# One core, attention then a gated MLP: the first loads, the turning of P, and the sorting of the first batch's V are done another way

## The chip, the cores and the metric
The kernel runs on one core of one Trainium2 chip. A core has five engines that work at the same time, each through its own queue in the order in which its instructions were issued: TensorE (PE; its weight loads are shown apart as PEld), VectorE (DVE), ScalarE (ACT), GpSimd (POOL) and SyncE (SP, which here only issues DMAs). Transfers run on 16 DMA engines and are issued from SP's or POOL's queue. The metric is the time of one execution in microseconds; less is better. Three runs of the kernel before gave 181.19, 182.1 and 182.74 us.

## The reference
Two layers, one after the other. The inputs are q, k and v of shape (4, 8, 768, 64), that is 4 batches, 8 heads, 768 positions, head size 64, and `sort_net` of shape (4, 8, 8, 8): for each batch and head an 8x8 matrix over the 8 blocks of 96 positions.

```python
P = sort_net
for _ in range(5):
    P = P - np.max(P, axis=-1, keepdims=True)
    P = np.exp(P)
    P = P / (np.sum(P, axis=-1, keepdims=True) + 1e-09)
    P = P / (np.sum(P, axis=-2, keepdims=True) + 1e-09)
k_sorted = np.einsum('bhij,bhjcd->bhicd', P, k_b)      # blocks mixed by P
v_sorted = np.einsum('bhij,bhjcd->bhicd', P, v_b)
scores = scale * np.matmul(q_b, k_sb.transpose(0, 1, 2, 4, 3))   # inside each block
attn = softmax(scores)
x = matmul(attn, v_sb), heads side by side              # (4, 768, 512)

h = np.maximum(x @ w_in, 0.0)                           # 512 -> 1024
u, v = halves of h
v_n = (v - mean) / sqrt(var + 1e-06)
v_s = np.einsum('ts,bsd->btd', w_spatial, v_n) + b_spatial[None, :, None]
out = (u * v_s) @ w_out                                 # 512 -> 512
```

All inputs are fp32 and so is the output; the kernel multiplies in bf16.

## The kernel before
All work is cut into units, Python functions named `u_XX`, and one long string, `ORDER`, lists the units in the order in which they are issued. `SC:3:0:2:0`, say, calls `u_SC` with those arguments. Each engine takes its own instructions in that order, so `ORDER` is the schedule of all queues; engines wait for each other only through the data. Where a unit's first argument is a number, it is the PSUM buffer, one of four (`ps0` to `ps3`), that it uses; an `A`, `D` or `P` after it says whether ACT, DVE or POOL takes the result out of PSUM or does the elementwise work.

The head. `IN` issues the loads of `sort_net` (tile `p_all`, all 32 batches and heads on 32 partitions) and of the bias `b_spatial` (tile `b_bc`, on all partitions) from SP. `ID` makes the identity matrix on POOL and a small mask from it on DVE (`mask16`). `L:q`, `L:k`, `L:v` load one batch's q, k or v; these loads are issued by POOL, because they cast from fp32 to bf16 on the way. The first batch's q comes in two halves of 64 partitions. `L:wv`, `L:wu`, `L:ws`, `L:wo` load the weights in the same way. `SK` is one round of the normalisation of P: an `Exp` on ACT and six DVE operations (lines 191 to 207). In the last round P is written out expanded, 16 times along the free axis, into `p_x`, half by DVE and half by POOL. `PR` and `PS` turn P by eight matmuls of `p_x` with the identity (line 218) so that P stands with blocks on partitions. From this `P0` on DVE (line 227) makes `pd[0]`, and `PC` and `PD` (POOL, line 239) make `pd[1]` to `pd[3]`: for each head a 128x128 matrix that mixes blocks by P. `DM` are dummy matmuls on a tile of zeros; their results are not used.

Attention. Positions are laid out so that partition p of a tile holds the six positions 6p to 6p+5; a block of 96 positions is 16 partitions. Per batch and pair of heads (`hp`, 0 to 3), and for batch 0 per half of the blocks (`ih`, 0 or 1): `QT` transposes q by 12 matmuls with the identity (line 276); `KT` mixes and transposes k by 12 matmuls with `pd` (line 291); `VM` mixes v by two matmuls (line 313) into `vm`, which still has 16 partitions to a block. `VC` then copies `vm` into `vb`, where each block stands on partitions 0 to 95, by four DMAs on SP for each half (line 328); this is the only step by which V gets from one layout to the other. `SC` makes the scores of four blocks and two heads (eight matmuls, line 341) and ACT takes their `Exp` (line 349). `AT` multiplies by `vb` (eight matmuls, line 364), and DVE divides by the sum of each row (lines 371 and 372). `XT` transposes the result (line 386).

The MLP. `VP` and `UP` are the two halves of the first projection (lines 405 and 446), with relu on ACT or DVE; `LN` and `LA` normalise; `WS` transposes the spatial weights (line 255), six times 128 columns in all; `SP` multiplies by them (line 458), adds the bias on DVE (line 464) and gates with u on DVE or POOL (line 470); `OP` is the last projection (line 479), followed by the output's DMA on SP (line 487).

In `ORDER` the first `AT` of batch 0 stands soon after `VC:0:0` and `VC:0:1`, and the units of neighbouring batches are interleaved, so that attention of one batch runs among the MLP of the batch before.

Of the kernel before, what the change touches and what calls it, by code (L numbers as in the profile page):

```python
# [21 lines left out]
SC:2:0:3:0 QT:0:D:0:3:1 SC:3:0:1:0 AT:1:0:2:0 PD:1:0:4 QT:2:A:0:0:1 AT:0:0:0:0 SC:3:0:3:1 SC:1:0:1:1
AT:2:0:3:0 AT:0:0:1:0 SC:3:0:2:1 XT:1:D:0:0:1 L:wo SC:2:0:0:1 XT:3:D:0:0:0 AT:0:0:1:1 PD:1:4:8
AT:1:0:3:1 WS:2:A:1 L:v:2:0:128 VP:3:D:0:0:1 L:k:2:0:128 WS:0:A:3 VP:2:A:0:2 VM:1:A:1:2 VM:3:A:1:0
UP:0:A:0:0:0 VM:2:A:1:1 AT:1:0:2:1 UP:3:A:0:1:0 AT:0:0:0:1 KT:1:A:1:2:2 XT:2:D:0:1:1 VM:3:A:1:3
WS:0:D:2 KT:1:A:1:0:2 KT:2:D:1:1:2 KT:3:A:1:3:2 VC:1:0 PD:3:4:8 VC:1:1 WS:0:D:4 WS:1:D:0 QT:2:A:1:2:2
QT:3:D:1:3:2 QT:0:A:1:1:2 QT:1:D:1:0:2 SC:2:1:2:0 XT:3:D:0:1:0 SC:0:1:3:1 SC:1:1:2:1 AT:2:1:2:0
# [499 lines left out]
```

## Time and profile before
| | us |
|---|---|
| median of three runs | 182.1 (181.19 to 182.74) |
| the profiled execution's own time | 184.14 |
| its span, first to last instruction | 182.0 |
| PE busy | 154.3 |
| PEld busy | 95.9 |
| DVE busy | 117.2 |
| ACT busy | 90.7 |
| POOL busy | 35.2 |
| mean granted clock of TensorE, share of full speed | 0.937 |

The profile is that of one execution, in which the hardware wrote down each instruction's start and end. A line of it names an engine, the line of the kernel, the operation, the tile that is written and those that are read. An idle time is followed by what ended it (`<-`). A busy PE is not PE at its best: matmuls are pipelined, and the clock that TensorE is granted can be half of full speed. The share of DMA is a mean over 16 engines and may exceed one, since transfers overlap.

### The profile page before, as it was taken

The page shows a single profiled execution, that of the slowest core. Times are in us where ns is not written, and L with a number is a line of the kernel's source. Part 1 is how long each engine was busy: PE and PEld are TensorE (multiplying, and loading weights), DVE is VectorE, ACT ScalarE, POOL GpSimd, SP SyncE. Part 2 cuts the span into 40 slices and gives each one's busy share as a digit, 9 for nine tenths or more (in the row PEclk, how much of TensorE's full clock was granted, in tenths as well). Part 3 has the DMA queues.
Part 4 walks back from the last instruction along what each step waited for, and adds up shares of the span by engine and source line. Part 5 has one row for each costly group of instructions (what it writes and reads, how often), then busy time and mean ns, then how long its engine had stood idle before and what let it go on. Part 6 is the DMA issues. An engine that isn't in the chain of part 4 may idle for free.

```text
span 182.0 us, 4057 instructions
## 1 busy us (share of the span) xinstructions
PE 154.3 (85%) x1716; PEld 95.9 (53%) x1728; DVE 117.2 (64%) x244; ACT 90.7 (50%) x133; POOL 35.2 (19%) x41
## 2 busy tenths in 40 slices
PE   0097943999956999999999999999999999999670
PEld 0064732866843467667555666666556664556220
DVE  3356941758843399758887669996777846657600
ACT  3040750729973289782468673445582256720050
POOL 7606980400410000026300000300000330003000
PEclk9999985569997599999999999999999999999997
DMA  3999999999999970550903415400054000332054
GB/s 86 185 204 204 210 226 244 206 204 205 203 231 237 204 124 4 82 100 0 162 14 115 174 60 87 97 0 4 0 199 150 0 0 4 115 119 111 0 190 158
DMA packets 21921, 22.38 MB, mean 123 GB/s; under 512 B 1040, under 2 KB 18704, under 8 KB 21904
## 3 DMA queue, kind: packets, MB, share of 16 engines
q0 software_dynamic: 14864, 12.19, 42.7%
q1 hardware_dynamic: 7040, 9.94, 18.6%
q8 instruction: 13, 0.21, 0.4%
q14 instruction: 4, 0.03, 0.0%
HBM read 24.78 MB, written 6.29 MB: 171 GB/s over the span
## 4 chain that ended last, share of the span: by engine, by line
PE 68%; DMA 13%; DVE 6%; ACT 4%; SPq 4%; issue 2%; POOL 1%; ACTq 0%; DVEq 0%; POOLq 0%
PE ps L458 15%; PE ps L405 12%; PE ps L446 12%; PE ps L479 9%; DMA vb<-vm 8%; PE ps L364 5%; DMA q_in<-in_q_dram 4%; SPq L328 4%; PE ps L341 4%; PE ps L386 3%; PE ps L313 3%; PE ps L276 2%; PE ps L291 2%; DVE z L464 2%; DVE gt L470 2%
## 5 line engine op out<-in xcount | busy, mean ns | idle before, releaser
L458 PE MATMUL ps<-wspT,v_sb 128*128 128x384 bf16 x192 | 33.2, 326 | 0.0
L470 POOL TENSOR_TENSOR gt<-z,u_sb 128x768 bf16<-128x768 f32 x7 | 11.5, 1645 | 103.2 <-DVE z L464 78.2
L349 ACT ACTIVATE ex<-ps 96x768 bf16<-96x768 f32 x32 | 24.5, 804 | 11.4 <-PE ps L341 11.3
L405 PE MATMUL ps<-w_in_sb,xT 128*128 128x512 bf16 x88 | 25.0, 417 | 0.6 <-issue 0.2
L458 PEld LDWEIGHTS <-v_sb 128*128 128x128 bf16 x192 | 18.1, 98 | 11.5
L479 PE MATMUL ps<-w_out_sb,gt 128*128 128x512 bf16 x92 | 22.2, 380 | 1.8 <-DVE gt L470 1.7
L446 PE MATMUL ps<-xT,w_in_sb 128*128 128x384 bf16 x128 | 23.3, 326 | 0.0
L372 DVE TENSOR_TENSOR x_sb<-ps,rec 96x512 bf16<-96x512 f32 x32 | 22.0, 687 | 1.1
L364 PE MATMUL ps<-vb,ex 96*128 96x65 bf16 x256 | 14.9, 203 | 8.6 <-DMA vb<-vm 8.6
L419 DVE BATCH_NORM_STATS2 stats<-v_sb 128x6 f32<-128x512 bf16 x24 | 16.3, 678 | 5.7 <-ACT v_sb L110 5.4
L104 ACT COPY o_sb<-ps 128x1024 f32<-128x1024 f32 x11 | 11.1, 1012 | 17.3 <-PE ps L479 15.9
L464 DVE TENSOR_TENSOR z<-ps,b_bc 128x768 f32<-128x768 f32 x16 | 15.2, 952 | 6.6 <-PE ps L458 6.6
L364 PEld LDWEIGHTS <-ex 96*128 96x128 bf16 x256 | 12.4, 104 | 12.7 <-issue 6.4
L110 ACT ACTIVATE u_sb<-ps 128x768 bf16<-128x768 f32 x16 | 13.0, 811 | 12.3 <-PE ps L446 12.0
L371 DVE RECIPROCAL rec<-ps 96x8 f32<-96x8 f32 x32 | 6.3, 197 | 15.9 <-PE ps L364 15.6
L276 PE MATMUL ps<-ident,q_in 128*64 128x128 bf16 (+1 forms) x240 | 8.4, 221 | 9.0 <-DMA q_in<-in_q_dram 9.0
L446 PEld LDWEIGHTS <-w_in_sb 128*128 128x128 bf16 x128 | 11.9, 98 | 7.7
L479 PEld LDWEIGHTS <-gt 128*128 128x128 bf16 x96 | 8.8, 97 | 11.9 <-DVE gt L470 2.3
L405 PEld LDWEIGHTS <-xT 128*128 128x128 bf16 x96 | 9.4, 106 | 10.6 <-issue 2.9
L104 ACT CAST qT<-ps 128x768 bf16<-128x768 f32 (+1 forms) x13 | 8.4, 675 | 10.5 <-PE ps L276 10.4
L104 ACT CAST kT<-ps 128x768 bf16<-128x768 f32 (+1 forms) x13 | 9.4, 727 | 8.2 <-PE ps L291 8.2
L276 PEld LDWEIGHTS <-q_in 128*64 128x64 bf16 (+1 forms) x240 | 6.9, 120 | 9.5 <-DMA q_in<-in_q_dram 9.0
(63 smaller groups left out, 190.8 us busy)
## 6 DMA issues: line engine op xcount, KB each, us to landing
out_dram<-o_sb SPq DMA_DIRECT2D x12, 512.0 KB, 2.8
vb<-vm SPq DMA_DIRECT2D x32, 99.0 KB, 4.8
v_in<-in_v_dram POOLq DMA_DIRECT2D x4, 768.0 KB, 17.9
k_in<-in_k_dram POOLq DMA_DIRECT2D x4, 768.0 KB, 20.4
q_in<-in_q_dram POOLq DMA_DIRECT2D x3, 768.0 KB, 24.6
wsp_nat<-in_moe_w_spatial_dram POOLq DMA_DIRECT2D x1, 1152.0 KB, 23.6
w_in_sb<-in_moe_w_in_dram POOLq DMA_DIRECT2D x2, 512.0 KB, 16.6
q_in<-in_q_dram POOLq DMA_DIRECT2D x2, 384.0 KB, 10.7
```

What stands on the lines that cost most here:

```text
L104: nc.scalar.copy(out=out, in_=in_)
L276: nc.tensor.matmul(t[hh * 64:hh * 64 + 64, g * n:(g + 1) * n], lhsT=st["q", b][lo:lo + n, 2 * hp + hh, g * D:(g + 1) * D], rhs=ident[lo:lo ...
L349: nc.scalar.activation(out=e[:, 0:2 * NI * BLK].rearrange("p (h c) -> p h c", h=2), in_=t[0:BLK, :, 0:NI * BLK], func=AF.Exp, scale=scale,)
L364: nc.tensor.matmul(t[:, hh, ii * VW:ii * VW + D + 1], lhsT=e[:, c:c + 128], rhs=vb[b % 2][:, ih * NI + ii, 2 * hp + hh, 0:D + 1], start=Tr ...
L372: nc.vector.tensor_mul(out=x_sb[:, :, hp * 128:hp * 128 + 128].rearrange("p i (h d) -> p h i d", h=2), in0=tv[:, :, :, 0:D], in1=_raw_ap(r ...
L405: nc.tensor.matmul(t[:, x, :], lhsT=st["xT", b][:, kc, n * 128:(n + 1) * 128], rhs=w_in_sb[:, kc, DH:DFF], start=(kc == 0), stop=(kc == KC ...
L419: nc.vector.bn_stats(out=stats, in_=v_sb[:, x, :])
L446: nc.tensor.matmul(t[:, x, 0:HW], lhsT=w_in_sb[:, kc, mc * 128:(mc + 1) * 128], rhs=st["xT", b][:, kc, ih * HW:(ih + 1) * HW], start=(kc = ...
L458: nc.tensor.matmul(t[:, x, 0:HW], lhsT=st["v_sb", b, n][:, mc * 128:(mc + 1) * 128], rhs=wspT[:, n, x * HW:(x + 1) * HW], start=(n == 0), ...
L464: nc.vector.tensor_add(out=z.rearrange("p (x c) -> p x c", x=2), in0=t[:, :, 0:HW], in1=b_bc.rearrange("p (x c) -> p x c", x=2),)
L470: eng.tensor_mul(out=gt, in0=z, in1=st["u", b, mc // 2][:, mc % 2])
L479: nc.tensor.matmul(t[:, x, :], lhsT=st["gt", b, mc][:, c * 128:(c + 1) * 128], rhs=w_out_sb[:, mc, :], start=(mc == 0), stop=(mc == FC - 1),)
```

## The change
Five things change, and `ORDER` is written anew from end to end.

- The first 64 partitions of batch 0's q are loaded by SP as fp32 into a new tile, `q_raw`, and cast on chip by the new unit `CQ`, a pair of heads at a time: three pairs on POOL, one on ACT. The second half of q is loaded as before.
- The first loads that POOL issues are K and V of batch 0. The bias `b_bc` is no longer loaded in `IN` but by a unit of its own, `BB`, which stands among batch 1's attention.
- The last round of `SK` writes P once, as bf16, and DVE turns it in two blocks of 32x32 (`p_t`). `PR` then expands it by eight matmuls with a constant tile of selections, `sel`, which `SX` makes on POOL from the identity. `p_x`, the expansion by DVE and POOL, and `PS` are gone. The mask is made by a unit of its own, `MK`.
- For batch 0 alone, `VM` and `VC` are replaced by `VT` and `VX`. `VT` mixes and transposes V as `KT` does K (12 matmuls, and a copy of 128x384); `VX` transposes it back block by block (four transposes on TensorE and a copy of 96x512), which writes `vb` directly. Batches 1 to 3 keep `VM` and `VC`.
- There are 10 dummy matmuls instead of 20.

```diff
     def u_IN():
         nc.sync.dma_start(out=p_all, in_=sort_net.rearrange("b h i j -> (b h) i j"))
-        nc.sync.dma_start(
-            out=b_bc, in_=_raw_ap(moe_b_spatial, 0, [[0, 128], [1, S]]))
+        nc.sync.dma_start(out=q_raw, in_=_raw_ap(q, 0, [[G * D, 64], [S * D, H], [1, G * D]]))
...
+    def u_BB():
+        nc.sync.dma_start(out=b_bc, in_=_raw_ap(moe_b_spatial, 0, [[0, 128], [1, S]]))
+
+    def u_SX():
+        nc.gpsimd.tensor_copy(
+            out=sel.rearrange("p i (j t) -> p i j t", t=TB),
+            in_=_raw_ap(ident, 0, [[ident.ap[0][0], BH], [NB, NI], [1, NB], [0, TB]]),
+        )
...
+    def u_CQ(eng, hp):
...
+        o, i = st["q", 0][0:64, 2 * hp:2 * hp + 2], q_raw[:, 2 * hp:2 * hp + 2]
+        if eng == "A":
+            nc.scalar.copy(out=o, in_=i)
+        else:
+            nc.gpsimd.tensor_copy(out=o, in_=i)
...
+        nc.vector.tensor_mul(
+            out=p_bf if int(last) else p_all, in0=p_all,
+            in1=_raw_ap(colsum, 0, [colsum.ap[0], [0, NB], colsum.ap[1]]),
+        )
         if int(last):
-            for ih, eng in enumerate((nc.vector, nc.gpsimd)):
-                eng.tensor_mul(
-                    out=p_x[ih],
...
+            nc.vector.transpose(
+                out=p_t.rearrange("p x y -> p (x y)"), in_=p_bf.rearrange("p i j -> p (i j)"))
 
     def u_PR(ps):
         st["pr"] = ps_tile(ps)[:, :, 0:NI * BH].rearrange("p x (i y) -> p x i y", i=NI)
...
+        for ih in range(2):
+            for ii in range(NI):
+                nc.tensor.matmul(
+                    st["pr"][:, ih, ii, :], lhsT=sel[:, ii, :], rhs=p_t[:, ih, :], start=True, stop=True)
...
+    def u_VT(ps, eng, hp, ih):
+        hp, ih = int(hp), int(ih)
+        t = ps_tile(ps).rearrange("p x c -> p (x c)")
+        mix_T(t, st["v", 0], 0, hp, ih * 64, 64)
+        st["vT", hp, ih] = att.tile([128, HW], BF16, name="vT", tag="vT", bufs=3)
+        copy(
+            eng,
+            st["vT", hp, ih].rearrange("p (x g) -> p x g", g=G),
+            t[:, 0:HW].rearrange("p (g x) -> p x g", g=G),
+        )
+
+    def u_VX(ps, eng, hp, ih):
+        hp, ih = int(hp), int(ih)
+        t = ps_tile(ps, BF16)
+        for ii in range(NI):
+            nc.tensor.transpose(
+                t[0:BLK, 0, ii * 128:(ii + 1) * 128], st["vT", hp, ih][:, ii * BLK:(ii + 1) * BLK], ident)
+        copy(
+            eng,
+            vb[0][:, ih * NI:(ih + 1) * NI, 2 * hp:2 * hp + 2, 0:D],
+            t[0:BLK, 0, 0:NI * 128].rearrange("p (i h d) -> p i h d", i=NI, h=2),
+        )
```

The beginning of `ORDER` after the change, up to the last unit of batch 1's `VC` and the first `AT` that reads it, so that the units between them can be counted:

```
IN ID L:k:0:0:128 MK L:v:0:0:128 SX SK:0 L:wv SK:0 CQ:P:2 CQ:A:3 SK:0 QT:0:A:0:3:0 SK:0 QT:1:A:0:2:0
DM:2:5:384 CQ:P:1 CQ:P:0 SK:1 L:q:0:64:128 IV:1 QT:3:A:0:0:0 QT:0:D:0:1:0 DM:1:5:384 PR:2 IV:0 PC:A
P0:0:4:8 P0:0:0:4 KT:3:A:0:3:0 KT:1:A:0:0:0 P0:1:4:8 L:wu PD:2:0:4 VT:0:A:1:0 P0:1:0:4 KT:2:D:0:2:0
PD:3:0:4 KT:3:A:0:0:1 KT:1:D:0:3:1 VT:0:D:2:0 SC:2:0:0:0 VT:3:D:0:0 PD:3:4:8 L:ws KT:1:D:0:1:0
SC:0:0:3:0 VX:2:D:1:0 L:v:1:0:128 L:k:1:0:128 VX:3:D:0:0 SC:1:0:2:0 KT:0:D:0:2:1 KT:2:A:0:1:1
QT:3:D:0:2:1 QT:1:A:0:1:1 QT:0:D:0:3:1 VT:2:A:3:1 SC:3:0:1:0 VX:1:D:2:0 AT:0:0:0:0 PD:1:0:4
VT:2:A:3:0 QT:1:A:0:0:1 VT:3:D:0:1 L:q:1:0:128 SC:2:0:1:1 VX:0:D:3:0 L:wo AT:1:0:2:0 VX:3:A:0:1
VX:0:A:3:1 AT:2:0:3:0 VT:3:A:1:1 VT:1:A:2:1 L:v:2:0:128 AT:0:0:1:0 SC:3:0:2:1 XT:2:D:0:0:1 SC:1:0:3:1
XT:0:D:0:0:0 L:k:2:0:128 VX:3:A:1:1 PD:1:4:8 WS:2:D:1 SC:1:0:0:1 WS:0:D:3 VX:3:A:2:1 L:q:2:0:128
WS:2:D:0 AT:1:0:1:1 WS:0:A:5 AT:3:0:0:1 VP:2:D:0:0:1 VM:1:A:1:2 VM:0:A:1:1 UP:3:A:0:0:0 VM:2:D:1:0
VM:1:A:1:3 VP:0:A:0:2 KT:3:A:1:2:2 KT:1:A:1:0:2 AT:2:0:3:1 UP:0:A:0:1:0 AT:3:0:2:1 KT:1:A:1:3:2
VC:1:1 XT:2:D:0:1:0 KT:0:A:1:1:2 QT:3:D:1:0:2 QT:1:A:1:3:2 QT:2:D:1:2:2 VC:1:0 QT:0:A:1:1:2 WS:3:D:2
SC:1:1:3:1 XT:2:D:0:1:1 SC:0:1:2:1 SC:3:1:1:0 AT:1:1:3:1 VP:2:A:0:5 SC:0:1:3:0 AT:1:1:2:1
```

More of the change, by code (lines that the diff above doesn't have):

```diff
@@ L22 @@
[L22 to L27, printed above, removed]
@@ L142, in alloc, with load @@
         st[x, b] = ld.tile([128, H, G * D], BF16, name=f"{x}_in", tag=x)
-    def load(x, b, lo, hi, first):
+    def load(x, b, lo, hi):
         src = {"q": q, "k": k, "v": v}[x]
-        if first:
+        if (x, b) not in st:
             alloc(b, x)
@@ L154, in u_L @@
         if what in ("q", "k", "v"):
-            load(what, int(a[0]), int(a[1]), int(a[2]), int(a[1]) == 0)
+            load(what, *(int(x) for x in a))
         elif what == "wv":
```

81 lines of the change are left out of this document (33 added, 48 removed).

## The prediction
> **What bounds the kernel now.** I read the page first, for the span and the row of the clock that was granted to TensorE in 40 slices, then the waits (us in total, times, longest) and the chain in order of time (start, length).
>
> ```profile
> span 182.0 us, 4057 instructions
> ...
> PEclk9999985569997599999999999999999999999997
> ```
>
> ```profile
> PE ps L364 <- DMA vb<-vm: 8.6, 9, 1.6
> ```
>
> ```profile
> 1.25 7.74 DMA q_in<-in_q_dram
> ...
> 22.88 7.66 DMA vb<-vm
> ...
> 52.88 6.04 DMA vb<-vm
> ```
>
> The execution took 184.14 us: this span and 2.14 us around it. TensorE waits for data three times: for the first half of q until 8.99, and twice for `vb`, the sorted V that DMAs copy from `vm`. After both waits for `vb` the clock row falls to 5. A table by stages prices that (columns: stretch and its length, busy time of PE, PEld, DVE, ACT and POOL with counts, granted clock, DMA share, GB/s):
>
> ```profile
> 17.86:24.95 7.09, 6.43 (x172) 5.11 (x172) 6.42 (x13) 4.87 (x8) 6.60 (x8) 1.00 1.20 210
> 24.95:30.60 5.65, 0.69 (x4) 0.36 (x5) 0.25 (x1) 0.88 (x2) 1.92 (x2) 0.58 1.17 242
> 30.60:37.50 6.90, 6.90 (x110) 6.14 (x110) 5.07 (x12) 3.60 (x5) 2.04 (x2) 0.50 1.30 213
> 37.50:39.70 2.20, 1.98 (x9) 0.92 (x8) 1.03 (x3) 0.80 (x1) 0.00 (x0) 0.53 1.32 208
> 39.70:52.00 12.30, 12.18 (x205) 9.00 (x205) 10.29 (x19) 10.27 (x15) 2.92 (x3) 1.00 1.30 205
> 52.00:56.70 4.70, 1.55 (x18) 0.92 (x19) 0.68 (x3) 1.46 (x2) 0.00 (x0) 0.99 1.24 244
> 56.70:63.20 6.50, 5.96 (x32) 2.62 (x30) 2.62 (x6) 2.55 (x5) 0.00 (x0) 0.50 1.30 215
> 63.20:161.00 97.80, 97.12 (x1031) 59.41 (x1040) 74.57 (x143) 59.21 (x84) 10.75 (x7) 1.00 0.31 72
> ```
>
> From 63.2 to 161 PE is busy 97.12 of 97.80: there it is the bound, and only work taken from PE would help. Before 63.2 it loses 4.96 us idle in the second row, 3.15 in the sixth, and runs at half clock for some 15 us. What half clock costs is seen in one group of score matmuls (line 341) and in the V projection (line 405), each slow and fast:
>
> ```profile
> 50.59 0.38 PE L341 MATMUL ps<-qT,kT 64*96 64x96 bf16 x8
> ...
> 57.44 0.56 PE L341 MATMUL ps<-qT,kT 64*96 64x96 bf16 x8
> ...
> 59.83 3.62 PE L405 MATMUL ps<-w_in_sb,xT 128*128 128x512 bf16 x8
> ...
> 75.15 1.89 PE L405 MATMUL ps<-w_in_sb,xT 128*128 128x512 bf16 x7
> ```
>
> 0.38 to 0.56 is a factor 1.5; 0.27 to 0.45 a matmul is 1.7. Of a busy microsecond at half clock 0.33 to 0.41 comes back.
>
> **Part 1, the head: -1.7 us.** Everything waits for the first `KT` matmul, at 17.86 now. Its chain is the five rounds of `SK`, then P into `pd`.
>
> ```profile
> 1.20 0.41 SPq L169 DMA_DIRECT2D b_bc<-in_moe_b_spatial_dram  x1
> ...
> 5.06 0.26 ACT L191 ACTIVATE p_all<-p_all 32x64 f32<-32x64 f32 x1 [2.46 <-DVE p_all L205]
> ...
> 9.61 0.48 ACT L104 CAST qT<-ps 128x384 bf16<-128x384 f32 x1 [4.29 <-PE ps L276]
> 9.98 0.25 ACT L191 ACTIVATE p_all<-p_all 32x64 f32<-32x64 f32 x1
> ...
> 10.46 5.96 PE L248 MATMUL ps<-warm 128*128 128x384 bf16 x20
> ...
> 11.74 0.26 ACT L191 ACTIVATE p_all<-p_all 32x64 f32<-32x64 f32 x1 [0.41 <-DVE p_all L205]
> ...
> 17.86 0.38 PE L291 MATMUL ps<-pd,k_in 128*64 128x64 bf16 x12 [0.94 <-DVE pd L227]
> ```
>
> ```profile
> b_bc<-in_moe_b_spatial_dram SPq DMA_DIRECT2D x1, 384.0 KB, 5.1
> ```
>
> ```profile
> L470 POOL TENSOR_TENSOR gt<-z,u_sb 128x768 bf16<-128x768 f32 x7 | 11.5, 1645 | 103.2 <-DVE z L464 78.2 <-DVE rec L371 25.0
> ```
>
> A round takes 11.74 - 9.98 = 1.76. The third `Exp` stands on ACT behind a copy that waits for q, so it starts at 9.98 instead of about 6.8. After the change the same place holds `CQ:A:3`, which waits for `q_raw`: the chain still hangs on q. `q_raw` is 768 KB from SyncE; `b_bc`, half of that, from the same queue at the same moment took 5.1 from its issue at about 1.2. So it lands between 6.3 (no dependence on size) and 11.4 (twice 5.1); I take 9.0, near the middle. Then the cast on ACT (0.8, as ACT's copies of that length), three rounds to 15.1, the DVE turn (a 32x64 operation, about 0.25), four `PR` matmuls and a `P0`: first `KT` at 16.2. The other way in is POOL: three `CQ:P` of 768 elements, between ACT's 0.8 and the 1.645 of POOL's two-input product, after `q_raw`. PE's queue holds two `QT` that need them, five dummy matmuls (0.3 each, from the 20 in 5.96) and then `PR`. At 1.645 POOL is done at 13.9 and `PR` starts at about 16.1, `KT` at 17.0; at 1.1, which I take as a middle, it is hidden behind the rounds. Bounds for the first `KT`: 13.5 to 18.6, a gain of 4.4 to a loss of 0.7.
>
> [...]
>
> Queued behind `CQ` on POOL are q's second half, `wu`, then three `PD`, and only then `ws` and batch 1's loads; K and V ahead of it go earlier than now. `SX` delays only `wv`. `b_bc` moves behind batch 1's `VC` on SP, long before `SP` wants it: nothing.
>
> **Part 2, batch 0 until its first V projection: -1.6 us.** Now that stretch runs from 17.86 to 37.5, 19.6 us. The change takes out eight DMAs on SP and four `VM`, and puts in eight `VT` and eight `VX`. On PE that is eight groups of 12 small matmuls and eight of four transposes, 128 in all, about 4.0 us by the first stage row (172 in 6.43, of which the eight long ones of `VM` took some 1.3), less those 1.3: +2.7. All PE units of the new stretch come to some 13.5 at full clock, so PE no longer sets its length. DVE and ACT do:
>
> ```profile
> L349 ACT ACTIVATE ex<-ps 96x768 bf16<-96x768 f32 x32 | 24.5, 804 | 11.4 <-PE ps L341 11.3
> ...
> L372 DVE TENSOR_TENSOR x_sb<-ps,rec 96x512 bf16<-96x512 f32 x32 | 22.0, 687 | 1.1
> ...
> L106 DVE COPY xT<-ps 128x768 bf16<-128x768 bf16 x12 | 6.6, 553 | 2.4 <-PE ps L386 2.3
> L371 DVE RECIPROCAL rec<-ps 96x8 f32<-96x8 f32 x32 | 6.3, 197 | 15.9 <-PE ps L364 15.6
> ...
> L106 DVE CAST kT<-ps 128x384 bf16<-128x384 f32 x5 | 2.6, 553 | 0.5 <-PE ps L291 0.5
> ...
> L104 ACT CAST kT<-ps 128x384 bf16<-128x384 f32 x3 | 1.4, 480 | 4.5 <-PE ps L291 4.5
> ```
>
> In the new order DVE has, up to `VP:2:D:0:0:1`: nine 384-element copies (`KT`, `QT`, `VT`) of 0.553, four `VX` at two thirds of the `xT` copy, 0.4 (an estimate), five 768-element `XT` and `WS` copies of 0.553, six `AT` of 0.197 + 0.687, and three `P0` of about 0.42: 5.0 + 1.6 + 2.8 + 5.3 + 1.25 = 15.9. ACT has eight `Exp` of 0.804, eleven copies of 0.48, four `VX` of about 0.6, a `WS` of 0.8 and `PC` of 0.4: 15.3. In the first stage row, with nothing to wait for, DVE was busy 6.42 of 7.09, 91%; 15.9 at that share is 17.5, and with ACT nearly as full I take 18.0. Bounds: PE alone at 13.5 (a gain of 6.1), and 20.5 (a loss of 0.9) if the two engines wait on each other in turn. The 8.6 us of waiting for `vb` thus goes, but mostly into DVE and ACT; that is why the step is worth so little here.
>
> **Part 3, from there to 63.2: -8.5 us.** Here the waits of batch 1 stand.
>
> ```profile
> 46.99 0.80 ACT L104 CAST vm<-ps 128x768 bf16<-128x768 f32 x1
> ...
> 47.86 5.63 SPq L328 DMA_DIRECT2D vb<-vm  x8
> ...
> 55.95 0.31 PE L364 MATMUL ps<-vb,ex 96*128 96x65 bf16 x5 [0.52 <-DMA vb<-vm]
> ...
> 58.97 0.43 PE L364 MATMUL ps<-vb,ex 96*128 96x65 bf16 x5 [0.50 <-DMA vb<-vm]
> ```
>
> Batch 1's copies start when the last `VM` is evicted (47.79); the first half is all there 8.2 us later and the second 11.2. PE ran out of other work at 52, some 4 us after. In the new order, after the last `VM` (`VM:1:A:1:3`), PE still has a single `VP`, four `KT`, two `AT`, a `UP`, two `XT`, four `QT`, a `WS` and three `SC` before the first `AT` of batch 1: an estimated 7.6 us of PE work (1.3 the `UP`, 0.9 the `VP`, 0.3 to 0.4 each of the small groups), and 8.6 of ACT's (ten operations of 0.8 and a shorter one). So it arrives at 8 to 9, when the first half is there, and the second half is wanted 5 us later, at 13 against 11.2. Both waits go, and what followed them: idle 0.22 + 0.12 + 3.15 + 0.54 = 4.0, and half clock 0.41 x (1.98 + 5.96) = 3.2. Three `WS` groups (six matmuls each) have moved into Part 2, 1.3 on PE. Sum 8.5. DVE at 10.29 of 12.30 in the fifth row leaves room. Bounds: 2 (waits remain) to 9.5.
>
> **Part 4, loads and the rest: +1.3.** DMA is saturated until past 63 (share 1.2 to 1.3 in the stage rows).
>
> ```profile
> 31.78 0.94 POOL L148 DMA_DIRECT2D q_in<-in_q_dram  x1 [4.91 <-PE ps L276]
> ...
> 71.33 0.53 PE L276 MATMUL ps<-ident,q_in 128*64 128x128 bf16 x12
> ```
>
> ```profile
> q_in<-in_q_dram POOLq DMA_DIRECT2D x1, 768.0 KB, 28.3
> ```
>
> Batch 2's q now lands at 60.1 and is wanted at 71.33, 11 us of slack, which the gain eats. But batch 0's eight copies, 0.8 MB, are gone from that traffic, some 3 us at 205 GB/s and more, while q's first half as fp32 takes the place of `b_bc`; so it lands at about 57 and is wanted at about 58: +0.5, from 0 to +4. The rest holds the same PE work to 0.4 us. At the end the last gate now writes `gt` 0, which the first `OP` reads first, where now two matmuls of 0.22 go ahead of it: +0.4.
>
> **Sum.** -1.7 - 1.6 - 8.5 + 1.3 = -10.5: 173.6 against this execution's 184.14. That one lies 2.04 above the median of 182.1. The stretches at half clock, which the change removes, are the likeliest part to differ between executions, so the new kernel should stand nearer its own sum: 173.0.
>
> **Rivals.** (a) Batch 1 still waits for `vb`, because DVE or loads push `VM` late or because the copies land later: 6 us of Part 3 come back less a little, 178.5. For: the copies go out one by one, and end 11 us after the last `VM` now. Against: 8 us of cover where there were 4. Chance 0.12.
>
> (b) In Part 2 PE is busy only 13.5 of 18 us, in short pieces. The row 24.95:30.60 shows that the clock falls within such a stretch of little work. If it falls once late in Part 2, and takes the 9 us to come back that it took before (30.6 to 39.7), most of that lies in Part 3, where PE is close to the bound: 9 x 0.41 less a little, 176.5. Chance 0.10. [...] Against: 6.43 of 7.09 kept it at 1.00 in the first row.
>
> (c) The slower side: the clock falls early in Part 2 and, with gaps everywhere, doesn't return until the first units of batch 2 are through. Then Part 2 takes 13.5 x 1.5 = 20.3 instead of 18.0, Part 3, with 15.5 of PE work in 17.2, takes 15.5 x 1.7 = 26.4, and some 7 us of PE work behind it lose 4: +15.5, 188.5. It is slower than before from about 29 us of PE work at half clock on. Against: the fifth row shows 12 us at full clock right after a fall. Chance 0.05.
>
> (d) `q_raw` is starved behind K, V and `wv`, 2.1 MB at the 205 GB/s of the stage rows, and lands at about 17 instead of 9: +8, 181.0. Against: `b_bc` wasn't starved. Chance 0.04.
>
> (e) DVE and ACT overlap so well that PE sets Part 2: 13.5 + 0.5, 4.0 less: 169.0. Chance 0.07.
>
> **Numbers.** My forecast, 173.0, has 0.62; its own bounds are 169 to 177. The range 168 to 179 takes in (a), (b) and (e). About 1% is what a measurement tells from no change, 180.3 to 183.9. Faster: 0.62 + 0.12 + 0.10 + 0.07 = 0.91; same: (d), 0.04; slower: (c), 0.05.
>
> **What would show it.** Part 1: the first `KT` matmul near 16, `q_raw` landing near 9, `PR` released by DVE. Part 2: the first `VP` some 18 us after the first `KT`, DVE about 90% busy in between, no wait for `vb`, clock 1.00. Part 3: no wait over 1 us for `vb` in batch 1. Part 4: no wait for q or K of batch 2 over 1 us. I am wrong if the clock row shows 5 anywhere after the head, if `vb` stays among the longest waits of PE, or if the first `KT` comes after 18.6.

## The result and the profile after
The changed kernel takes 174.96 us, the median of four runs (173.83 to 175.95); the kernel before, run beside it, 182.42. The ratio is 0.960, with a 95% interval of 0.951 to 0.969. The forecast was 173.0, with a range of 168 to 179. Executions of one kernel differ by 1 to 3% here, and a trace is that of one of them; where a traced execution lies off its median, its own time is given. The traced one of the changed kernel took 175.73 (before: 184.14), with a span of 173.7 (182.0).

The page of the kernel after, its span and the row of the granted clock:

```profile
span 173.7 us, 4271 instructions
...
PEclk9999975569999999999999999999999999999996
```

The clock row still falls to 5 after the head, in one stretch instead of two, and this stretch stands where no wait for `vb` is. The head, in the timeline (start, length):

```profile
7.84 0.83 ACT L203 CAST q_in<-q_raw 64x768 bf16<-64x768 f32 x1 [3.48 <-DMA q_raw<-in_q_dram]
...
7.87 2.36 POOL L205 CAST q_in<-q_raw 64x768 bf16<-64x768 f32 x3 [3.20 <-DMA q_raw<-in_q_dram]
...
15.43 0.71 PE L303 MATMUL ps<-pd,k_in 128*64 128x64 bf16 x24 [0.92 <-DVE pd L239]
```

The first `KT` starts at 15.43 (17.86 before). The stages behind it, each row a stretch with its length, busy time of PE, PEld, DVE, ACT and POOL (with counts of instructions), granted clock, DMA share and GB/s:

```profile
15.43:20.11 4.68, 4.53 (x157) 3.94 (x157) 4.05 (x11) 3.66 (x7) 4.68 (x6) 1.00 1.27 206
20.11:21.81 1.70, 0.00 (x1) 0.00 (x1) 0.52 (x1) 0.43 (x1) 1.70 (x2) 1.00 1.24 207
21.81:26.64 4.83, 4.83 (x128) 4.23 (x128) 3.04 (x7) 3.85 (x7) 1.72 (x3) 0.75 1.16 212
26.64:27.73 1.09, 0.00 (x1) 0.00 (x0) 0.18 (x1) 0.05 (x1) 0.00 (x0) 0.50 1.23 199
27.73:37.87 10.14, 10.14 (x140) 9.28 (x139) 6.14 (x13) 5.70 (x10) 4.85 (x5) 0.50 1.31 204
37.87:54.79 16.92, 16.16 (x233) 10.48 (x233) 13.10 (x26) 13.30 (x20) 1.81 (x2) 1.00 1.26 228
54.79:157.00 102.21, 101.78 (x1066) 62.60 (x1074) 78.77 (x151) 59.64 (x84) 9.07 (x6) 1.00 0.40 91
```

Rows two and four are new: PE does nothing, and DVE and ACT do little (0.52 and 0.43 of 1.70 us, 0.18 and 0.05 of 1.09). The chain of waits names no releaser for them; "issue" is time in which the engine waited for nothing that the profile shows:

```profile
1.19 6.63 DMA q_raw<-in_q_dram
...
20.11 1.70 issue
...
26.64 1.09 issue
...
45.68 5.57 DMA vb<-vm
```

What was left of the waits for `vb`, 0.6 us, stands at the end of the row of its group:

```profile
L399 PE MATMUL ps<-vb,ex 96*128 96x65 bf16 x256 | 13.8, 201 | 1.7 <-issue 1.1 <-DMA vb<-vm 0.6
```

Part by part, in us of the two traces. Part 3 ends at the two groups of score matmuls that follow `VP:3:D:0:3:4` in both orders; they start at 63.38 before and at 54.79 after. (The prediction cut at 37.5 and 63.2, and so had 19.6 and 25.7 for Parts 2 and 3 before.)

| | before | predicted | after |
|---|---|---|---|
| Part 1, to the first `KT` | 17.9 | 16.2 | 15.4 |
| Part 2, to the first `VP` | 19.8 | 18.0 | 22.4 |
| Part 3, to these score matmuls | 25.8 | 17.2 | 16.9 |
| Part 4, to the end of the span | 118.6 | 119.9 | 118.9 |

Part 3 came as predicted; Part 2 became 2.7 us longer where 1.6 less was predicted. That is 4.4 more than the forecast and 1.9 beyond its outer bound of 20.5. The question is what stands in Part 2.

### The profile page after: what moved, and what is told of

It is laid out like the page before. It is cut to its first block, busy times and chain, and to the rows that moved or that the text cites. A ratio compares the mean times of both kernels' runs of the same rounds, so it can differ in the third digit from the quotient of the medians.

```text
span 173.7 us, 4271 instructions
## 1 busy us (share of the span) xinstructions
PE 151.8 (87%) x1827; PEld 97.8 (56%) x1838; DVE 120.1 (69%) x252; ACT 93.5 (54%) x140; POOL 34.1 (20%) x42
## 4 chain that ended last, share of the span: by engine, by line
PE 74%; DMA 9%; DVE 9%; issue 3%; ACT 2%; SPq 1%; ACTq 0%; DVEq 0%
PE ps L493 17%; PE ps L440 11%; PE ps L481 11%; PE ps L514 10%; PE ps L399 5%; PE ps L376 5%; DMA q_raw<-in_q_dram 4%; PE ps L303 3%; PE ps L421 3%; DMA vb<-vm 3%; PE ps L288 2%; PE ps L336 2%; PE ps L267 2%; DMA out_dram<-o_sb 2%; PE ps L348 1%
## 5 line engine op out<-in xcount | busy, mean ns | idle before, releaser
L384 ACT ACTIVATE ex<-ps 96x768 bf16<-96x768 f32 x32 | 24.7, 803 | 17.9 <-PE ps L376 17.5
L505 POOL TENSOR_TENSOR gt<-z,u_sb 128x768 bf16<-128x768 f32 x6 | 9.8, 1638 | 100.4 <-DVE z L499 76.6
L514 PE MATMUL ps<-w_out_sb,gt 128*128 128x512 bf16 x92 | 21.7, 379 | 2.3 <-DVE gt L505 2.1
L440 PE MATMUL ps<-w_in_sb,xT 128*128 128x512 bf16 x89 | 22.2, 379 | 0.4
L106 ACT COPY o_sb<-ps 128x1024 f32<-128x1024 f32 x10 | 10.1, 1013 | 18.4 <-PE ps L514 14.3
L112 ACT ACTIVATE u_sb<-ps 128x768 bf16<-128x768 f32 x15 | 12.1, 809 | 7.8 <-PE ps L481 7.4
L481 PEld LDWEIGHTS <-w_in_sb 128*128 128x128 bf16 x128 | 11.8, 98 | 7.6
L399 PE MATMUL ps<-vb,ex 96*128 96x65 bf16 x256 | 13.8, 201 | 1.7 <-issue 1.1
L440 PEld LDWEIGHTS <-xT 128*128 128x128 bf16 x96 | 8.7, 97 | 9.2
L376 PEld LDWEIGHTS <-kT 64*96 64x96 bf16 x256 | 8.2, 128 | 4.9 <-issue 3.7
L376 PE MATMUL ps<-qT,kT 64*96 64x96 bf16 x256 | 10.8, 219 | 0.1
L112 ACT ACTIVATE v_sb<-ps 128x1024 bf16<-128x1024 f32 (+1 forms) x9 | 8.4, 928 | 4.6 <-PE ps L440 4.6
```

The source lines that it names most:

```text
L112: nc.scalar.activation(out=out, in_=in_, func=AF.Relu)
L376: nc.tensor.matmul(t[0:BLK, hh, ii * BLK:(ii + 1) * BLK], lhsT=kT[rows, i * BLK:(i + 1) * BLK], rhs=qT[rows, i * BLK:(i + 1) * BLK], start ...
L384: nc.scalar.activation(out=e[:, 0:2 * NI * BLK].rearrange("p (h c) -> p h c", h=2), in_=t[0:BLK, :, 0:NI * BLK], func=AF.Exp, scale=scale,)
L399: nc.tensor.matmul(t[:, hh, ii * VW:ii * VW + D + 1], lhsT=e[:, c:c + 128], rhs=vb[b % 2][:, ih * NI + ii, 2 * hp + hh, 0:D + 1], start=Tr ...
L440: nc.tensor.matmul(t[:, x, :], lhsT=st["xT", b][:, kc, n * 128:(n + 1) * 128], rhs=w_in_sb[:, kc, DH:DFF], start=(kc == 0), stop=(kc == KC ...
L481: nc.tensor.matmul(t[:, x, 0:HW], lhsT=w_in_sb[:, kc, mc * 128:(mc + 1) * 128], rhs=st["xT", b][:, kc, ih * HW:(ih + 1) * HW], start=(kc = ...
```

## The experiments

**Three theories of Part 2.** Between the two stops PE executed exactly 128 matmuls, each with its weight load: 256 instructions. An instruction queue is listed among the DMA queues of the page (`q8 instruction: 14, 0.23`): 14 packets of 16 KB. Theory 1: PE's instructions come in blocks of 256 through the same DMA engines as the loads, so that PE runs out of instructions among small matmuls while DMA is saturated; the half clock follows from the stops. Theory 2: the clock falls because PE waits briefly and often for DVE and ACT. Theory 3: DVE and ACT set Part 2 anyhow, and stops and clock cost nothing.

In the diffs below, lines of `ORDER` are cut down to the part that changes, and `...` marks what is left out.

**1. The fetch by itself.** Only matmuls of the size of one in `KT`, first without loads, then under them; the rest of the kernel is taken out.

```diff
+def u_A(n):   # and u_B, the same on another line
+    st["t"] = ps_tile(0)
+    for i in range(int(n)):
+        nc.tensor.matmul(st["t"][(i % 2) * 64:(i % 2) * 64 + 64, 0, 0:64], lhsT=warm[:, 0:64], rhs=warm[:, 64:128],
+                         start=True, stop=True)
...
+IN A:768 GT L:k:0:0:16 GB L:k:0:16:128 L:v:0:0:128 L:q:0:0:128 L:wv L:wu L:ws L:k:1:0:128 L:v:1:0:128 L:q:1:0:128 L:wo
+B:1024 OZ
```

> Measures the disputed cost by itself; it leaves the whole computation out and writes zeros. Phase A: 768 matmuls of the size of a KT matmul (128 partitions, 64 columns), each with its weight load, on a tile of zeros, while no transfer runs. Phase B: 1024 of the same, while ten loads of the kernel (K, V, q and weights) saturate DMA. Theory 1 (TensorE's instructions are fetched 256 at a time, that is 128 such matmuls, through the same DMA engines as the loads): in A 128 matmuls take about 4.1 us (12 take 0.38 in the kernel) and no stop is over 0.3 us; in B PE stops for 1 to 2 us with no releaser after every 128 matmuls, so 128 take 5.5 to 6.5 us, and the granted clock falls to about 0.5 for a part of it. Theories 2 and 3 (the stops come from something else in the kernel): B runs like A, 4.1 us per 128, without stops.

PE's timeline, two blocks without loads (line 496, DMA share 0.02) and two under them (line 510, share 1.2 to 1.3):

```profile
13.97 2.22 PE L496 MATMUL ps<-warm 128*64 128x64 bf16 x128 [1.51 <-issue]
17.43 2.21 PE L496 MATMUL ps<-warm 128*64 128x64 bf16 x128 [1.24 <-issue]
...
38.20 3.62 PE L510 MATMUL ps<-warm 128*64 128x64 bf16 x128 [2.29 <-issue]
44.12 3.62 PE L510 MATMUL ps<-warm 128*64 128x64 bf16 x128 [2.30 <-issue]
```

A stop after every 128 matmuls, as theory 1 has it, and a period that doesn't depend on the work: 44.12 - 38.20 = 5.92 us for 256 instructions under loads. My "no stop without loads" was wrong: there the period is 17.43 - 13.97 = 3.46, and these matmuls, at 17 ns, are through in 2.2. In the kernel after, PE resumes at 21.81 and at 27.73 behind the two stops: the period is 5.92 there too. The 128 matmuls between them take 4.8, which hides 3.46 and not 5.92. The DMA records of that trace show the fetch itself: a packet of 16 KB on the instruction queue from 19.49 to 20.43 and the next from 25.45 to 26.39, and PE resumes 1.4 and 1.3 us behind their ends.

**2. The kernel without the loads of that time.** Its readers take other data (`src` gives batch 0's tile for batch 1, for q and K alike), and batch 2's loads are issued later; all instructions on PE, DVE and ACT stay.

```diff
-L:wu
-L:ws
-L:v:1:0:128 L:k:1:0:128
-L:q:1:0:128
-L:wo
...
-rhs=st["v", b][:, 2 * hp + hh, :]
+rhs=src("v", b)[:, 2 * hp + hh, :]
...
-t[:, 0, c * 128:(c + 1) * 128], wsp_nat[:, c, n * 128:(n + 1) * 128], ident)
+t[:, 0, c * 128:(c + 1) * 128], w_in_sb[:, c % KC, DH + (n % 4) * 128:DH + (n % 4 + 1) * 128], ident)
```

> The kernel after, with the loads left out that run during batch 0's attention: wu, ws, wo and batch 1's q, K and V (their readers use wv and batch 0's q, K and V in their place), and batch 2's loads issued some 20 units later; so its output is another one. Every other instruction is kept. Theory 1 (instruction fetch behind loads): the two stops of 1.70 and 1.09 us go, the clock stays at 1.00 from the first KT to the first VP, and that stretch takes 18 to 19 us where it took 22.4. Theory 2 (the clock falls from PE's short waits on DVE and ACT): no long stop, but the clock falls to 0.5 in the stretch, which takes 20.5 to 22.5. Theory 3 (DVE and ACT set the stretch whatever PE does): clock 1.00, and still about 22.

Part 2 takes 17.2 us, from 15.79 to 32.95, with one stop of 0.35. Theory 3 falls. But the time as a whole (one execution) is 175.11, no better than the kernel after. PE's timeline:

```profile
18.69 0.53 PE L301 MATMUL ps<-pd,v_in 128*64 128x64 bf16 x12
...
26.34 0.25 PE L397 MATMUL ps<-vb,ex 96*128 96x65 bf16 x3 [0.35 <-issue]
...
32.95 1.89 PE L438 MATMUL ps<-w_in_sb,xT 128*128 128x512 bf16 x7
...
48.12 0.31 PE L397 MATMUL ps<-vb,ex 96*128 96x65 bf16 x5 [1.11 <-DMA vb<-vm]
```

The last line is where most of the 5 us went: PE comes to batch 1 earlier, the waits for `vb` are back (2.0 in all), half clock follows from 49.2 to 52.6, and Part 3 takes 20.2 where it took 16.9. Part 1 is 0.4 and Part 4 1.2 longer. The first line shows something else. A `VT` of 12 matmuls takes 0.53 here and 0.38 at full clock in the kernel after (where one at half clock, at 24.76, takes 0.53 as well), while the clock row says 1.00; from 22.95 on it takes 0.38 here too. The trace's record of the clock begins with its first change, a rise at 21.9 in this run; the row fills what lies before with 1.00. The pace of the matmuls tells what it was.

**3. The same work, 128 instructions further on.**

```diff
-IN ID L:k:0:0:128 MK
+IN DM:3:64:64 ID L:k:0:0:128 MK
```

> The kernel after with 64 dummy matmuls of 64 columns more at the very start, where TensorE waits for q anyway (about 4 us, over before q is there). The work of every later stage is the same; only the count of instructions ahead of it differs, by 128. Theory 1 (fetch of 256 instructions at a time): the stops leave the places where they are now (after 5 of 12 matmuls of KT:2:A:0:1:1, and after 5 of 8 of AT:1:0:2:0) and stand 64 matmuls earlier: none or a short one inside VT:3:D:0:0, since that block is fetched during the head, one of 0.5 to 2 us after the first matmul of VX:1:D:2:0, and maybe one after 5 of 8 of XT:2:D:0:0:1. Theories 2 and 3: the stops stay in the same units or are spread. The time: 173 to 176.

```profile
24.20 0.33 PE L336 MATMUL ps<-ident,vT 128*96 128x128 bf16 x3 [0.87 <-issue]
...
30.95 0.40 PE L421 MATMUL ps<-ident,x_sb 96*128 96x96 bf16 x3 [1.71 <-issue]
```

The stops stand after the first matmul of `VX:1:D:2:0` (three of four are left) and after five of eight of `XT:2:D:0:0:1`, the very matmuls that were named. That settles where the stops come from. The time is the surprise: 172.44 median of five, ratio 0.943 (0.936 to 0.950), with work added and none removed, against 0.960 for the kernel after. The traced execution is the longest, at 177.03, so its trace doesn't show why the others are faster. Where the blocks end differs, and so may what the clock does at the start; which of them gives the gain stays open.

**4. Batch 0's V by `VM` and `VC` again,** with all `VT` and `VX` out.

```diff
-VT:0:A:1:0 P0:1:0:4
+P0:1:0:4 VM:0:A:0:1
...
-VT:0:D:2:0 SC:2:0:0:0 VT:3:D:0:0 PD:3:4:8 L:ws
+VM:0:D:0:2 SC:2:0:0:0 VM:3:D:0:0 VM:2:A:0:3 VC:0:0 VC:0:1 PD:3:4:8 L:ws
...
-VX:2:D:1:0
```

> The kernel after, with batch 0's V again by VM and VC (four VM, eight DMAs) in place of VT and VX; all else is kept. If VT and VX are worth what the waits for vb cost before (5.0 us idle in batch 0 and the half clock that followed), 178 to 181 us against 175.0 for the kernel after. Rival: VT and VX only turned the wait into instruction fetch and half clock, so that both ways cost the same: 174 to 176.

```profile
29.61 0.54 PE L399 MATMUL ps<-vb,ex 96*128 96x65 bf16 x2 [4.74 <-DMA vb<-vm]
```

179.72 us, ratio 0.993 (0.989 to 0.996); Part 2 takes 25.7. So the wait of 4.7 and the half clock behind it are what `VT` and `VX` save: 3.2 us of Part 2 and 3.6 of the span in the two traces, 4.8 between the two medians.

**5. The kernel before, with only batch 1's `VM` and `VC` earlier.**

```diff
-VP:3:D:0:0:1 L:k:2:0:128 WS:0:A:3 VP:2:A:0:2 VM:1:A:1:2 VM:3:A:1:0
-UP:0:A:0:0:0 VM:2:A:1:1 AT:1:0:2:1
...
-XT:2:D:0:1:1 VM:3:A:1:3
...
-VC:1:0 PD:3:4:8 VC:1:1
...
+VP:3:D:0:0:1 VM:1:A:1:2 VM:0:A:1:0 L:k:2:0:128 VM:2:A:1:1 VM:1:A:1:3 VC:1:0 VC:1:1 WS:0:A:3 VP:2:A:0:2
+UP:0:A:0:0:0 AT:1:0:2:1
```

> The kernel before, with only batch 1's VM and VC issued earlier: all four VM right after the first VP, ahead of the second VP and the first UP, VC straight behind. If order alone buys Part 3 of the prediction, the two waits of batch 1 for vb (3.6 us of idle time) and the half clock behind them go: 175.5 to 178 against 182.4. Rival: the copies are slow because DMA is saturated by loads and by batch 0's copies, so the waits stay: 180.5 to 183.

```profile
37.62 0.63 PE L405 MATMUL ps<-w_in_sb,xT 128*128 128x512 bf16 x1
...
58.13 0.56 PE L341 MATMUL ps<-qT,kT 64*96 64x96 bf16 x16
```

No wait for `vb` is left in batch 1, and Part 3 takes 58.13 - 37.62 = 20.5 us where it took 25.8. The time is 178.86, ratio 0.987 (0.975 to 0.998): a gain, but less than I expected. In the traces a good half of Part 3's 8.8 us is order alone. By the medians order alone is worth less, 2.9 us (181.77 to 178.86, run side by side); the traced execution of the kernel before lies 2 us above its median.

**6 to 8. The head freed from q, `KT` and `VT` made whole, and both.** In the first, all rounds of `SK` go ahead of what needs q:

```diff
-SK:0 L:wv SK:0 CQ:P:2 CQ:A:3 SK:0 QT:0:A:0:3:0 SK:0 QT:1:A:0:2:0
-DM:2:5:384 CQ:P:1 CQ:P:0 SK:1 L:q:0:64:128 IV:1 QT:3:A:0:0:0 QT:0:D:0:1:0 DM:1:5:384 PR:2 IV:0 PC:A
+SK:0 L:wv SK:0 SK:0 SK:0 CQ:P:2 CQ:A:3 CQ:P:1 CQ:P:0 SK:1 QT:0:A:0:3:0 QT:1:A:0:2:0
+DM:2:5:384 L:q:0:64:128 IV:1 DM:1:5:384 PR:2 IV:0 PC:A QT:3:A:0:0:0 QT:0:D:0:1:0
```

> The kernel after, with all rounds of SK on ACT ahead of the casts and copies that need q, and the four q units behind PR. If the third Exp's wait for q still holds the head, the first KT comes at 12.2 to 13.2 instead of 15.4, and K, which lands at 11.1, just allows it; the total falls by 1 to 2.5, to 172.5 to 174. Rival: loads set the pace behind it (V lands at 15.0, the second half of q at 19.5), so the gain is given back in the next stretch: 174.5 to 175.5.

P was turned at 11.8 us instead of 14.1, but I had put `PR` on PE behind two `QT`, which wait for q until 8.95, and ten dummies, and `P0` on DVE behind a copy that waits for a `QT`. The first `KT` came at 15.28, 0.15 earlier. The time is 175.46, ratio 0.957 (0.950 to 0.963): with the first `KT` where it was, neither expectation was tried. Its stops stand at the same two matmuls as in the kernel after, whose count of instructions up to there it shares:

```profile
21.35 0.31 PE L303 MATMUL ps<-pd,k_in 128*64 128x64 bf16 x7 [0.92 <-issue]
...
27.29 0.27 PE L399 MATMUL ps<-vb,ex 96*128 96x65 bf16 x3 [1.92 <-issue]
```

In the second, `KT` and `VT` of batch 0 take 128 columns at a time:

```diff
-mix_T(t, st["v", 0], 0, hp, ih * 64, 64)
+mix_T(t, st["v", 0], 0, hp, 0, 128)
...
-KT:3:A:0:3:0 KT:1:A:0:0:0 P0:1:4:8
...
-KT:3:A:0:0:1 KT:1:D:0:3:1
...
+P0:1:4:8 KT:3:A:0:3:2 P0:0:0:4 P0:1:0:4 KT:1:D:0:0:2
```

> The kernel after, with batch 0's KT and VT made whole (128 columns instead of twice 64): 96 matmuls and 192 PE instructions fewer between the first KT and the first VP, and eight copies of 768 in place of sixteen of 384. Theory 1: one stop fewer there, and the stretch falls from 22.4 to 17.5 to 19.5 us, if the clock stays; total 170 to 173. Theory 2 (clock falls from short waits on DVE and ACT): the clock still falls, 21 to 22.5 us, total 174 to 175. Theory 3 (DVE and ACT set the stretch): it gains only the copies that they save, about 1 us, total 174.

> Whole KT and VT and the freed head together. If the two gains are independent, 168 to 171.5. If loads set the pace once the first KT is early, no better than the better one of the two.

Neither has a stop over 0.25 us in Part 2. But whole `KT` and `VT` alone take 178.75 us (176.09 to 179.91; ratio 0.968, 0.957 to 0.978). In the traced execution, the longest of the four, Part 2 takes 21.2: the clock rose only at 22.7, and it fell again at 26.1 after nothing but waits of at most 0.5 us:

```profile
22.72:26.13 3.41, 2.60 (x65) 2.08 (x64) 2.48 (x5) 2.27 (x4) 1.76 (x3) 1.00 1.17 212
26.13:29.55 3.42, 2.98 (x49) 2.64 (x49) 1.31 (x3) 2.17 (x4) 1.72 (x2) 0.50 1.22 205
```

With the head as well it is 172.76 (ratio 0.943, 0.937 to 0.949), though that head gains nothing by itself, and Part 2 takes 17.3 (first row), Part 3 19.4, again with 1.3 of waits for `vb` and 3.4 us at half clock (second):

```profile
15.21:32.48 17.27, 15.12 (x329) 13.41 (x329) 12.95 (x27) 12.38 (x19) 11.99 (x13) 0.90 1.25 207
32.48:51.83 19.35, 17.69 (x235) 11.20 (x234) 13.60 (x26) 13.52 (x20) 1.81 (x2) 0.91 1.26 228
```

So stops aren't needed for half clock. Theory 1 explains the stops and not the whole fall. The traces of two kernels with the same order of Part 2 differ by 4 us in it, and the clock differs with it: half up to 22.7 and for three windows after 26.1 in the one, half for a single window near the start in the other.

**9. A version meant to be best.** `PR` and `P0` ahead of the rest of q, dummies up to the first `KT`, two of batch 1's `VM` ahead of the first `VP`:

```diff
+IN DM:3:12:384 ID L:k:0:0:128
...
+SK:1 QT:0:A:0:3:0 QT:1:A:0:2:0
+DM:3:4:384 PR:2 DM:0:2:384 L:q:0:64:128 IV:1 IV:0 PC:A P0:0:4:8 P0:1:4:8 KT:3:A:0:3:2 P0:0:0:4 P0:1:0:4 QT:0:A:0:1:0
...
+VM:1:A:1:2 VM:0:D:1:1 VP:2:A:0:0:1 VM:1:D:1:0 VM:0:A:1:3 UP:3:A:0:0:0
```

> A version meant to beat both kernels: whole KT and VT as in the run before; the rounds of SK and then PR stand ahead of everything that waits for q on DVE, ACT and (but for two QT) PE, with dummy matmuls on PE up to the first KT; and two of batch 1's VM ahead of the first V projection, whose relu goes to ACT, so that VC starts earlier. If the head is held only by the order of the queues, the first KT comes at 12.5 to 13.5 (15.2 in the version with both changes); if the waits for vb there (1.3 us, and some 4 us at half clock behind them) come from VM's late evictions, they go. Both: 167 to 170 against 172.8. If loads (V at 15, the second half of q at 19.5, batch 1's V at about 31) set the pace, 171 to 173.

The first `KT` comes at 13.68, but the time is 176.27 (ratio 0.968, 0.960 to 0.977), and Part 2 takes 23.3 without a stop. The clock row shows why:

```profile
PEclk9955985599999999999999999999999999999997
```

**Theory 4: what the clock counts.** In all the traces a stretch at half clock that the end of the recording doesn't cut lasts a multiple of 3.41 us: 13.7 and 6.8 before, 13.7 after, and 3.4, 6.8, 10.2, 13.7, 17.1 and 23.9 among the experiments.

So I took the clock to be set anew every 3.41 us, divided each trace into windows of this length, from the recorded changes on, and counted for each its matmuls' columns times the share of the 128x128 array (the largest weights in the traces are 128*128) that their weights fill; a `KT` matmul of 64 columns with 128x64 weights counts 32. In the 14 traces, 561 windows at full clock: the 34 with under 2,500 were all followed by half clock, of 12 between 2,500 and 2,920 six, and of the 515 above none. From half clock: 34 windows under 2,600, none followed by full clock; nine up to 3,010, three of them; 23 above, all. That is a count made after the fact, and the next run was to try it.

By this count a stop (theory 1) and short waits (theory 2) bring the fall alike, by the work that they keep out of a window; no run here tells it from another measure that goes with it. The same fall stands near the end of six traces (experiments 2, 3, 6, 7, 10 and 12): one window at half clock, and a Part 4 of 120.1 to 120.6 us where it is 118.9 without, as in the kernel after. That alone is 1.2 to 1.7 us of difference between traces.

**10. Dummies among batch 0's `KT`, `VT` and `QT`.**

```diff
+def fill(t):
+    for _ in range(1):
+        nc.tensor.matmul(t[:, 512:896], lhsT=warm[:, 0:128], rhs=warm[:, 0:384], start=True, stop=True)
```

> The kernel after with 20 dummy matmuls of 384 columns (whole array, on a tile of zeros, into the unused half of the PSUM tile), one in each KT, VT and second-half QT of batch 0; their results are not used, and everything else is kept. Theory 4, from the runs so far: every stretch at half clock lasted a multiple of 3.41 us (13.6 and 6.7 before, 13.5 after, 10.2, 6.8 and 3.4 in the experiments); counting for each such window its matmuls' columns times the share of the 128x128 array that their weights fill, windows at full clock with under some 2,650 were followed by half clock and those above (but for one of about 2,530) were not, and back from half clock it took some 2,900 to 3,100, which KT and VT, with half the array, can't reach. So the dummies (about 1,400 more in a window) keep the clock at 1.00 between the first KT and the first VP, although the two stops of the instruction fetch stay, and the stretch takes 18.5 to 20.5 us where it took 22.4; total 172 to 174. Rival (the stops or short waits themselves make the clock fall, not the amount of work): half clock as in the kernel after, the stretch 22 to 25 us, total 174.5 to 177.

187.23 us, 1.7% slower than the kernel before (ratio 1.017, 1.005 to 1.028), and outside both expectations: Part 2 takes 28.8. The clock was at half already when the first `KT` began (12 matmuls in 0.53, and the first recorded change is a rise at 39.6), so it couldn't be held, and each dummy cost 0.4 us of PE at half pace. Timeline and windows:

```profile
20.29 0.53 PE L305 MATMUL ps<-pd,k_in 128*64 128x64 bf16 x12
20.76 0.50 PE L533 MATMUL ps<-warm 128*128 128x384 bf16 x1
```

```profile
22.52:25.93 3.41, 3.41 (x48) 2.35 (x46) 1.74 (x4) 1.61 (x2) 1.41 (x2) 1.00 1.16 211
25.93:29.35 3.42, 3.42 (x59) 2.15 (x59) 1.23 (x4) 1.28 (x2) 0.00 (x0) 1.00 1.25 205
29.35:32.76 3.41, 3.41 (x49) 2.13 (x46) 0.89 (x2) 1.37 (x3) 0.00 (x0) 1.00 1.31 204
```

PE is busy without a gap for over 20 us and the clock doesn't rise (the row's 1.00 is the filling again): these three windows hold 2,650, 2,510 and 2,470. These half-array matmuls in a row, dummies included, didn't make enough work at half clock to get out. So a busy window isn't enough; in the kernel after, too, PE was busy 10.14 of the 10.14 us from 27.73 and stayed at half clock. Whether dummies would hold a clock that is up was not tried by this. In experiment 1 PE was busy only 2.2 of 3.4 us in windows that stayed at full clock, with 4,096 in each.

**11 and 12. Dummies in the head, and batch 1's V earlier.** Batch 1's V is loaded ahead of the spatial weights; its `VM` and `VC` stand ahead of the first `VP`, and the `WS` that stood there behind it.

```diff
+IN DM:3:30:384 ID L:k:0:0:128
...
+DM:3:8:384 PR:2 DM:0:4:384
...
+PD:3:4:8 L:v:1:0:128
...
+L:ws L:k:1:0:128
...
+VM:2:D:1:0 AT:1:0:1:1 VM:0:A:1:3 AT:3:0:0:1 VC:1:1 VC:1:0 VP:2:D:0:0:1 WS:1:A:1 WS:0:A:3 UP:3:A:0:0:0 WS:2:D:0
+WS:1:A:5 VP:0:A:0:2
```

> A second try at a version that beats both kernels. As the one before (whole KT and VT, SK and PR ahead of all that waits for q), with dummy matmuls through the head and two of 256 columns in each KT, VT and second-half QT of batch 0; batch 1's V is loaded ahead of the spatial weights, its four VM and both VC stand ahead of the first V projection, and the four WS that stood there come behind it, as cover for the copies into vb. Theory 4: clock 1.00 from the first KT (13.5 to 14) on, no fetch stop over 0.3 us, the first VP some 17 to 18 us later, at 31 to 32, and no wait of 0.5 us or more for vb in batch 1: 165 to 169. If the dummies don't hold the clock, or delay the copies out of PSUM as much as they save, 172 to 176.

172.2 us (171.95 to 174.08), ratio 0.943 (0.935 to 0.950). No wait for `vb` is left, and Part 3 takes 16.2. In the traced execution, the longest, the clock fell at the first `KT`, for two windows, and `KT`'s and `VT`'s copies waited for the dummies, over 7.5 us in all on ACT and DVE; Part 2 took 23.4. Without the dummies in `KT` and `VT`, and with five dummies more in the head:

```diff
-DM:3:8:384 PR:2 DM:0:4:384
+DM:3:11:384 PR:2 DM:0:6:384
...
-        if b == 0:
-            fill(t)
```

> The version before without the dummies in KT and VT (their copies out of PSUM waited for them, by up to 3 us at a time); those in the four second-half QT stay, and there are five dummies more in the head. In that run the only window with less than 2,650 of work ahead of the fall (2,624, from 10.7 to 14.1 us) was followed by half clock, and every window after the clock came back held more than 3,300 and was not. Theory 4: with five dummies of 384 more the window around the first KT holds over 3,500, so the clock is at 1.00 from the first KT on; the QT stretch holds about 3,000 to 3,700, so it stays there until batch 1; the first VP comes 16 to 18 us after the first KT, and the total is 167 to 170.5. If the clock falls in the first KT or among the QT as in the versions without dummies, one to three windows of 3.41 us at half clock and 172 to 175.

174.23 us, ratio 0.953 (0.944 to 0.961); the traced execution is the longest of four, at 175.65. Some windows of that trace:

```profile
14.97:18.38 3.41, 2.85 (x86) 2.55 (x80) 2.76 (x4) 2.74 (x5) 3.41 (x5) 1.00 1.26 206
18.38:21.79 3.41, 1.86 (x40) 1.37 (x38) 2.04 (x4) 1.61 (x2) 3.41 (x5) 1.00 1.28 205
21.79:25.21 3.42, 3.42 (x50) 2.29 (x50) 1.51 (x3) 1.28 (x2) 0.71 (x1) 0.50 1.31 205
```

The head went as theory 4 says: four windows of 7,400, 4,000, 4,400 and 4,800 at full clock, none followed by half. Then the `QT` of the second half came before their data, among other short waits:

```profile
21.05 0.37 PE L287 MATMUL ps<-ident,q_in 64*64 64x64 bf16 x12 [0.63 <-DMA q_in<-in_q_dram]
```

That window holds 1,830, and four windows at half clock follow. A head that is 1.7 us earlier meets loads that aren't, and in this trace pays with the clock. The best three versions (3, 8 and 11) stand at ratios of 0.943, some 1.8% below the kernel after (0.960), and can't be told apart from each other.

## Why the prediction was right, and where it wasn't
**The step that failed: Part 2's "18.0", and with it the sentence that PE "no longer sets its length".** Measured 22.4. Two terms were missing. The first is the stops of the instruction fetch, 1.70 + 1.09 = 2.8 us, shown by experiments 1 and 3: the change put 128 small matmuls into a stretch where DMA is saturated (share 1.16 to 1.31), and I had costed them by their duration alone. The second is half clock from 24.2 to 37.9: the units from the second stop to the first `VP` take 10.1 us in the kernel after and 6.6 (26.34 to 32.95) in experiment 2, at full clock; 3.5 us. The two together are more than the 4.4 that were missed; my 18.0 was 0.7 to 0.8 above the 17.2 and 17.3 of experiments 2 and 8, so the sums of DVE and ACT were not too small.

**Rival (b) is what happened**, at a chance of 0.10: a fall in Part 2. It came in the middle and not late, and lasted four windows, where I took 9 us from one instance before. The window before it held 2,510, with 1.02 us of the first stop in it; at its own pace, 2,511 in 2.39 us of busy time, that stop took some 1,070. So in this trace the stop probably made the clock fall; experiments 7 and 9 show falls in Part 2 without one. What brings the fall in general stays open, beyond the count of theory 4. By my own condition ("if the clock row shows 5 anywhere after the head") I was wrong about Part 2.

**Part 3, -8.5, was right** at 16.9 against 17.2, and the cause as well: experiment 5 gets 5.2 of it from the order alone. But it was right with luck, in a kernel whose Part 2 is late. PE comes to the first `AT` of batch 1 only 6.7 us after the first copy is issued (I took 8 to 9 of work). In the kernel after the first half's copies are there after 7.5 us, so that a wait of 0.6 is all that is left. In experiments 2 and 8, with Part 2 about as long as I predicted, PE comes after 6.8 and 6.7 us, the copies need 9.3 and 8.6, and Part 3 takes 20.2 and 19.4. So two errors probably offset each other: had Part 2 been 18, Part 3 would have been some 2 to 3 longer, and the sum about where it is.

**Part 1, -1.7, gave -2.4.** `q_raw` landed at 7.82, not 9.0, and the copies on POOL took 0.79 each, not 1.1. One price was left out there: ten dummy matmuls instead of 20 was costed at nothing. In four experiments with this same head (2, 4, 7 and 10) the clock was still at half when the first `KT` began (24 of its matmuls took 0.86 us in experiment 2, 0.71 in the kernel after); in the trace of the kernel after it rose at 14.0, just in time.

**Part 4, +1.3, gave +0.3**: q of batch 2 landed at 58.2 and was wanted at 61.8; nothing was late.

The sum, -10.5 predicted, is -8.3 in the traces: -2.43 + 2.68 - 8.84 + 0.28. The range held because its upper part was made of such rivals.

## What to carry to other kernels
Count PE's instructions, not only their time: where DMA is full, 256 of them cost a floor of about 5.9 us here, and replacing a few DMAs by many small matmuls spends that. Price half clock in whole windows of 3.41 us, and ask of each window whether its matmuls fill enough of the array (by the count of theory 4 no window above 2,920 was followed by a fall); a PE that is busy with half-array matmuls may stay at half clock, as it did for over 20 us in experiment 10. And when a stage is made earlier, look again at the wait behind it: a forecast that adds up stages is right only if each of them starts when it is said to.
